# An attention and two-MLP kernel on one core: another mix of tile kinds, other ranks for the planner, and the first shifts all planned

## The chip, the cores and the metric

One NeuronCore of a Trainium2 chip runs the whole kernel. The metric is the device time of one execution in microseconds. Engines: PE (TensorE, products), DVE (VectorE), ACT (ScalarE), POOL (GpSimd) and SP, whose queue issues nearly all DMAs.

## What is computed

Three steps in a row, all in float32: attention with a bucket mask (2 batches, 8 heads, 768 rows, 64 columns a head), a gated MLP with a token shift, and a low-rank token mix followed by a channel MLP.

```python
def _attn_ref(q, k, v, proj):
    ...
    mask = q_bucket[:, :, :, None] == k_bucket[:, :, None, :]
    scores = scale * np.matmul(q, k.transpose(0, 1, 3, 2))
    scores = np.where(mask, scores, -1000000000.0)
    scores = scores - np.max(scores, axis=-1, keepdims=True)
    attn = np.exp(scores)
    attn = attn / (np.sum(attn, axis=-1, keepdims=True) + 1e-09)
    return np.matmul(attn, v).astype(np.float32)

def _moe_ref(x, mu_k, mu_r, w_k, w_v, w_r):
    ...
    xk = mu_k * x + (1.0 - mu_k) * x_prev
    xr = mu_r * x + (1.0 - mu_r) * x_prev
    k = np.maximum(xk @ w_k, 0.0)
    v = k * k @ w_v
    r = 1.0 / (1.0 + np.exp(-(xr @ w_r)))
    return (r * v).astype(np.float32)

def _moe2_ref(x, U, V, w_ch1, w_ch2):
    xt = x.transpose(0, 2, 1)
    h = xt @ U @ V
    u = x + h.transpose(0, 2, 1)
    ch = np.maximum(u @ w_ch1, 0.0) @ w_ch2
    return (u + ch).astype(np.float32)
```

The weights of both MLPs arrive as 64-bit floats and are turned into two float32 parts (high and low) on the chip.

## The kernel before

**Attention.** 16 heads (2 batches of 8) with 6 tiles of 128 rows each, so 96 tiles. For each tile PE makes the scores (`scores`, L514), DVE the row maximum, scale and bias (L524 to L534), ACT the exponentials into a float32 tile `p` (`exps`, L537). Then `p` has to be transposed and multiplied by V. There are two ways:

- The tiles 1 and 4 of each head (`PE_TILES`, L23; 32 in all) are transposed on PE (`flip`, L560), copied out of PSUM in float32 by ACT or DVE (`flip_out`, L568) and multiplied by V in float32 (`weighted`, L573, the product of L581).
- The other 64 are cast to fp16 on POOL or ACT (`part1`, L542), the remainder is subtracted on POOL (`part2`, L546), both parts are transposed by one DMA from SP's queue (`transp`, L554) and multiplied as fp16 (the product of L587, 18 for a tile).

V is scaled by a power of two that is found for a group of `VG` = 4 heads (L470 to L497).

**The order of the attention** comes out of a planner. Every step is an `Op` (L50) with the engines that can do it and a cost on each, the ops it follows, the buffers (`Slot`) it takes and frees, and a rank: its place in the list of tiles plus a number from the table `DUE` (L24). `Plan.order` (L76) plays the ops with these costs; among those that are ready it takes the lowest rank first. The sequence that results is the order in which each engine's instructions are written. Wherever the play leaves PE without work, `idle_products` (L330) adds small products of no use, about 0.85 of the gap's length.

**Handover.** The planned part also holds the conversion of the first `JOBS` = 8 weight tiles, and for batch 0 of the gated MLP the shift `mu * x + (1 - mu) * x_prev` of both halves of r, the products of r, and the shift of the first half of k. A shift is four steps for each of 4 column chunks: `shift_scaled` and `shift_sum` (L705, L720; ACT or DVE, and DVE), `shift_high` (L726, ACT) and `shift_low` (L740, POOL or DVE). The shift of the second half of k is written behind the planned part, between the first unit and the others (L1112, L1113).

**The MLPs.** From there the order is written out by hand. A unit of the gated MLP is `k` (L779, 12 products of 384 columns), `k_act` (L787: relu and square on ACT, a product on POOL), `k_low` (L794, DVE) and, one unit later, `v` (L798, 9 products of 512 columns). With the units run the ticks (L254 to L263): each loads, scales, joins and splits weight tiles, one step of five tiles in a row. The list of tiles is w_r (4), then w_k and w_v in turn (16), U, V in two halves, then the channel MLP's 32. The channel mix (`Channel`, L850) ticks in its first of three groups.

## Time and profile before

| | us |
|---|---|
| median of 3 runs (728.45 to 728.57) | 728.49 |
| the profiled execution | 728.76 |
| its span, first to last instruction | 727.0 |
| PE busy in the span | 707.1 |
| DVE, ACT, POOL busy | 440.6, 385.2, 351.1 |

The span is what the trace covers. Matmul ends are modelled, so a busy PE may still hold small gaps. Times in the rows count from the span's start. In a row of a group "x32 | 47.4, 274" means 32 instructions, 47.4 us during which at least one of them ran, and 274 ns for one from its start to its modelled end.

### The profile page before, as it was taken

The numbers are of one execution on the slowest core, as the hardware profiler recorded it, in microseconds if no ns is written. First come the engines' busy times: TensorE is split into PE (matmuls) and PEld (weight loads), VectorE is DVE, ScalarE is ACT, GpSimd is POOL, SyncE is SP. The second block draws the span as 40 slices with busy tenths as digits, with TensorE's granted clock in tenths as the row PEclk, the third lists the DMA queues.
The fourth block names the chain that finished last, engine by engine and source line by source line (L and its number), as shares of the span: only waits on it lengthen the run. The fifth ranks groups of instructions, "written<-read, shape, count | busy, mean of one in ns | idle before, by whom it ended". The sixth has DMA issues, their size and how long they took to land.

```text
span 727.0 us, 12722 instructions
## 1 busy us (share of the span) xinstructions
PE 707.1 (97%) x4907; PEld 612.1 (84%) x4907; DVE 440.6 (61%) x791; ACT 385.2 (53%) x651; POOL 351.1 (48%) x309
## 2 busy tenths in 40 slices
PE   9899999999999998999999999999999999999997
PEld 8798999999999886889788888778888888888886
DVE  7987888677776656898879978655532111321112
ACT  5887888688878666666478566434421001110100
POOL 5998888787969855566357544613300000000000
PEclk9999999999999999899999999999999999999999
DMA  7899899996987961322013332323201000010001
GB/s 189 194 177 198 190 198 205 167 175 148 174 182 144 208 114 58 116 75 92 2 59 115 116 114 63 125 77 109 65 0 59 1 0 1 1 58 1 0 1 58
DMA packets 140715, 73.23 MB, mean 101 GB/s; under 512 B 116832, under 2 KB 134064, under 8 KB 140656
## 3 DMA queue, kind: packets, MB, share of 16 engines
q1 hardware_dynamic: 140512, 72.24, 43.2%
q8 instruction: 38, 0.62, 0.3%
q10 hardware_dynamic: 144, 0.20, 0.1%
q14 instruction: 21, 0.17, 0.1%
HBM read 37.10 MB, written 3.15 MB: 55 GB/s over the span
## 4 chain that ended last, share of the span: by engine, by line
PE 75%; DVE 8%; POOL 5%; DMA 4%; issue 4%; ACT 3%; SPq 0%; POOLq 0%; ACTq 0%; DVEq 0%
PE ps L807 9%; PE pt L807 9%; PE ps L809 9%; PE pt L809 9%; PE pt L808 9%; PE ps L808 9%; PE pt L581 3%; DMA pT<-p 3%; PE pt L587 3%; PE ps L521 3%; POOL p L180 2%; PE ps L522 2%; PE pt L453 2%; DVE w L180 2%; PE pt L415 1%
## 5 line engine op out<-in xcount | busy, mean ns | idle before, releaser
L882 DVE SCALAR_TENSOR_TENSOR hl<-pt,hl 128x512 fp32r<-128x512 f32 x48 | 33.2, 691 | 170.9 <-ACT hl L881 170.9
L881 ACT ACTIVATE hl<-pt 128x512 fp32r<-128x512 f32 x48 | 28.7, 598 | 185.1 <-PE pt L809 185.1
L809 PE MATMUL ps<-w,hl 128*128 128x512 f32 x288 | 114.3, 397 | 3.3 <-DVE hl L796 3.1
L807 PE MATMUL ps<-w,hl 128*128 128x512 f32 x288 | 115.7, 402 | 0.1
L808 PE MATMUL ps<-w,hl 128*128 128x512 f32 x288 | 113.9, 395 | 0.0
L180 POOL TENSOR_TENSOR cx<-cx,raw 128x512 int32<-128x512 int32 (+2 forms) x55 | 80.4, 1461 | 65.2 <-DVE cx L233 59.2
L180 POOL TENSOR_TENSOR p<-p,p 128x768 f16<-128x768 f32 x64 | 108.0, 1693 | 7.8 <-ACT p L389 5.9
L526 DVE TENSOR_REDUCE nm<-ps 128x1 f32<-128x768 f32 x96 | 90.5, 952 | 17.3 <-PE ps L522 15.9
L540 ACT ACTIVATE p<-ps,nm 128x768 f32<-128x768 f32 x96 | 92.9, 988 | 11.7 <-DVE nm L534 10.3
L807 PE MATMUL pt<-ut,w 128*128 128x512 f32 x192 | 75.6, 394 | 0.0
L809 PE MATMUL pt<-ut,w 128*128 128x512 f32 x192 | 75.0, 391 | 0.0
L808 PE MATMUL pt<-ut,w 128*128 128x512 f32 x192 | 75.0, 391 | 0.0
L521 PE MATMUL ps<-xk,xq 76*128 76x384 f32 x192 | 70.6, 368 | 1.9 <-ACT p L540 1.2
L809 PEld LDWEIGHTS ps<-w,hl 128*128 128x128 f32 x288 | 54.5, 189 | 19.2 <-DVE hl L796 7.1
L807 PEld LDWEIGHTS ps<-w,hl 128*128 128x128 f32 x288 | 54.5, 189 | 14.1 <-issue 1.7
L180 DVE TENSOR_TENSOR w<-cx,w 128x512 fp32r<-128x512 f32 (+2 forms) x52 | 61.2, 1177 | 8.2 <-ACT w L273 7.7
L522 PE MATMUL ps<-yk,yq 128*128 128x384 f32 x192 | 65.1, 339 | 0.0
L808 PEld LDWEIGHTS ps<-w,hl 128*128 128x128 f32 x288 | 54.6, 190 | 10.3
L229 DVE SCALAR_TENSOR_TENSOR raw<-raw 128x512 uint32<-128x512 uint32 (+2 forms) x55 | 54.2, 985 | 0.0
L180 POOL TENSOR_TENSOR sq<-sq 128x384 f32<-128x384 f32 x32 | 32.0, 1000 | 38.2 <-ACT hl L791 37.2
L391 POOL CAST p<-p 128x768 f16<-128x768 f32 x49 | 41.3, 843 | 17.1 <-ACT p L540 15.8
L587 PE MATMUL pt<-v,pT 128*128 128x65 f16 (+1 forms) x1152 | 45.7, 194 | 2.5 <-DMA pT<-p 2.5
(181 smaller groups left out, 1511.5 us busy)
## 6 DMA issues: line engine op xcount, KB each, us to landing
raw<-in_moe_w_ch_dram SPq DMA_DIRECT2D x32, 512.0 KB
raw<-in_moe_w_k_dram SPq DMA_DIRECT2D x8, 512.0 KB
raw<-in_moe_w_v_dram SPq DMA_DIRECT2D x8, 512.0 KB
nk<-in_k_dram SPq DMA_DIRECT2D x16, 192.0 KB
nv<-in_v_dram SPq DMA_DIRECT2D x16, 192.0 KB
nq<-in_q_dram SPq DMA_DIRECT2D x15, 192.0 KB
xk<-yk SPq DMA_DIRECT2D x15, 192.0 KB
xq<-yq SPq DMA_DIRECT2D x15, 192.0 KB
```

Source lines behind the costliest of these rows:

```text
L180: eng.tensor_tensor(out=out, in0=a, in1=b, op=op)
L229: nc.vector.scalar_tensor_tensor(out=raw[:, :, 0], in0=raw[:, :, 1], scalar=0x80000000, in1=raw[:, :, 0], op0=ALU.bitwise_and, op1=ALU.bit ...
L391: (nc.vector if e == "dve" else nc.gpsimd).tensor_copy(dst, src)
L521: nc.tensor.matmul(s_ps[:, j, 0:G], d["xq"][:, qc], d["xk"][:, c], start=True, stop=False)
L522: nc.tensor.matmul(s_ps[:, j, 0:G], d["yq"][:, qc], d["yk"][:, c], start=False, stop=True)
L526: nc.vector.tensor_reduce(out=nm[:, 0:1], in_=tl[n]["s"][:, :, 0:G], axis=AX.XY, op=ALU.max, negate=True)
L540: nc.scalar.activation(p, tl[n].pop("s")[:, :, 0:G], AF.Exp, bias=nm[:, 2:3], scale=nm[:, 1:2])
L587: nc.tensor.matmul(o[:, 0:d], pT[:, part, kt, :], V[:, kt, a, 0:d], start=(kt == 0 and (part, a) == (0, 0)), stop=(kt == NT - 1 and part = ...
L807: nc.tensor.matmul(o, sh, mh, start=first, stop=False)
L808: nc.tensor.matmul(o, sh, ml, start=False, stop=False)
L809: nc.tensor.matmul(o, sl, mh, start=False, stop=last)
L882: nc.vector.scalar_tensor_tensor(out=hl[:, 1], in0=self.o, scalar=0.0, in1=f(hl)[:, 0], op0=ALU.max, op1=ALU.subtract)
```

## The change

The table `MODES` gives each tile of a head a kind, one string for each batch: D goes by DMA as fp16 parts, W is flipped on PE and stays float32, and F is new: flipped on PE, then split out of PSUM into fp16 parts by ACT (high) and DVE (rest) and multiplied as D is. That makes 64 tiles D, 24 W (16 in batch 0, 8 in batch 1) and 8 F (all in batch 1). All ranks of `DUE` are new, and several costs that the planner plays with. Six weight tiles instead of eight are converted in the attention; the ticks take over two tiles earlier in the list, with two more ticks in the channel mix. The V groups are of 2, 2, 4, 4 and 4 heads. The shift of k's second half is planned too; its buffers `xh2` lie where the preparation of the heads had its own, which are given back behind the last scores. The first MLP's units go in the order 0, 1, 2, 3 instead of 0, 2, 1, 3.

```diff
-PE_TILES = (1, 4)
-DUE = {"ld": -28.3, "h": 7, "lo": 111.2, "tr": -11.5, "es": -25.5, "xs": 92.5, "z": -68.8, "bits": 0,
...
+MODES = ("DDWDDW", "DDFDDW")
+DUE = {"ld": -252.8, "h": -1.6, "lo": 280.8, "tr": 133.2, "es": -299.3, "xs": -53.6, "z": -552.9,
...
-JOBS = 8
-VG = 4
+JOBS = 6
+GROUPS = (2, 2, 4, 4, 4)
...
+        scored.append(n)
+        if len(scored) == NH * NT:
+            prep_s.close()
+            late["xh2"] = pool(mix_s, "xh2", bufs=4)
...
+    def mode(n):
+        return MODES[n // (NT * H)][n % NT]
...
+    def flipped(n, part):
+        return tl[n]["pT"][:, part].rearrange("p (j i) c -> p j (i c)", j=NG), tl[n]["f"][:, :, 0:G]
+
+    def flip_part1(n):
+        pT_tile(n)
+        p1, src = flipped(n, 0)
+        nc.scalar.activation(p1, src, AF.Copy)
+
+    def flip_part2(n):
+        p1, src = flipped(n, 0)
+        minus("dve", flipped(n, 1)[0], src, p1)
+        tl[n].pop("f")
...
-        if t in PE_TILES:
+        if mode(n) == "W":
             pT, v = tl[n].pop("pF"), NV[i % len(NV)]
...
+            if kind == "F":
+                p1 = add({"act": 0.83}, lambda e, n=n: flip_part1(n), [fl], n, "f1", [pT_s])
+                got = add({"dve": 0.97}, lambda e, n=n: flip_part2(n), [p1], n, "f2", free=[f_s])
...
-            avs.append(add({"pe": 0.9 if on_pe else 0.62}, lambda e, n=n: weighted(n), [got, v0_of[i] if on_pe else v2], n, "av",
+            avs.append(add({"pe": 1.32 if kind == "W" else 0.56}, lambda e, n=n: weighted(n), [got, v0_of[i] if kind == "W" else v2], n, "av",
...
-    for j, (s, g, c) in enumerate(todo := mx0.todo[0:3 * KD]):
+    for j, (s, g, c) in enumerate(todo := mx0.todo):
         a_s = Slot("sq")
         if c == 0:
-            x_s = [Slot("xh") for _ in range(KD)]
+            far = (s, g) == ("k", 1)
+            x_s = [Slot("xh2" if far else "xh") for _ in range(KD)]
...
-    u1 = [0, 2, 1, 3, *range(4, U1 - 3), U1 - 2, U1 - 3, U1 - 1]
+    u1 = [*range(U1 - 3), U1 - 2, U1 - 3, U1 - 1]
...
-    while mix.todo or mix.begun:
-        shifts(mix, nc.gpsimd if len(mix.todo) % 2 else None)
...
-                if m in (8, 10, 12):
+                if m in (4, 6, 8, 10, 12):
                     tick()
```

How the instructions stand now, at three places. First DVE near the end of the attention, where the last tiles' maxima (`nm<-ps`) are taken. In the rows `pF<-ps` is the float32 copy of a flipped tile, `xs_a` a shift, `y_150` or `y_153` a result of r, `raw` and `cx` a weight tile in conversion, `rl` the row sums. Before:

```order
L526 TENSOR_REDUCE nm<-ps 128x1
L391 COPY pF<-ps 128x768
L530 TENSOR_SCALAR nm<-nm 128x1
L534 TENSOR_SCALAR nm<-nm 128x1
L229 SCALAR_TENSOR_TENSOR raw<-raw 128x512
L233 TENSOR_SCALAR cx<-cx 128x512
L710 MEMSET xs_a 128x1
L391 COPY y_150<-pt 128x512
```

After:

```order
L538 TENSOR_REDUCE nm<-ps 128x1 x2
L738 MEMSET xs_a 128x1
L542 TENSOR_SCALAR nm<-nm 128x1 x2
L546 TENSOR_SCALAR nm<-nm 128x1 x2
L750 SCALAR_TENSOR_TENSOR xs_a<-xT,mu_k,xs_a 128x384 x2
L232 SCALAR_TENSOR_TENSOR raw<-raw 128x512
L236 TENSOR_SCALAR cx<-cx 128x512
L181 TENSOR_TENSOR pT<-ps,pT 128x768
L750 SCALAR_TENSOR_TENSOR xs_a<-xT,mu_k,xs_a 128x384
L622 TENSOR_SCALAR rl<-pt,vsc 128x6
```

`pT<-ps,pT` is the second part of an F tile, which stands here instead of a float32 copy, and k's shifts (`mu_k`) have come in among the last tiles.

Second ACT at the handover. `xT<-pt` is the last copy of the attention's result, `sq<-pt` the relu of a unit of the first MLP, `hl<-sq` its square, `xs_a` and `xh` are shifts, `w`, `cx` and `raw` weights. Before:

```order
L273 ACTIVATE w<-cx 128x512
L790 ACTIVATE sq<-pt 128x384
L791 ACTIVATE hl<-sq 128x384
L224 ACTIVATE cx<-raw 128x512
L225 ACTIVATE raw<-raw 128x512
L716 ACTIVATE xs_a<-xT,omu_k 128x384
L737 ACTIVATE xh<-xs_a 128x384
L716 ACTIVATE xs_a<-xT,omu_k 128x384
L737 ACTIVATE xh<-xs_a 128x384 x3
L273 ACTIVATE w<-cx 128x512
L790 ACTIVATE sq<-pt 128x384
```

After:

```order
L744 ACTIVATE xs_a<-xT,omu_k 128x384
L765 ACTIVATE xh<-xs_a 128x384
L392 ACTIVATE xT<-pt 128x384 x2
L765 ACTIVATE xh<-xs_a 128x384
L276 ACTIVATE w<-cx 128x512
L818 ACTIVATE sq<-pt 128x384
L819 ACTIVATE hl<-sq 128x384
L227 ACTIVATE cx<-raw 128x512
L228 ACTIVATE raw<-raw 128x512
L276 ACTIVATE w<-cx 128x512
L818 ACTIVATE sq<-pt 128x384
```

The shifts that stood between the relu of the first unit and that of the second are now ahead of the first; one high part stands behind the last copy of the attention.

Third DVE in the first MLP, from the eleventh unit's `hl<-sq` on, the low part of a unit's result. `raw` and `cx` are conversions (128x512 a full weight tile, 128x192 the matrix U, 32x384 a half of V), `w<-cx` the split of a tile. Before:

```order
L796 TENSOR_TENSOR hl<-sq,hl 128x384
L180 TENSOR_TENSOR w<-cx,w 128x512
L710 MEMSET xs_a 128x1
L718 TENSOR_SCALAR xs_a<-xT,omu_r 128x127
L718 TENSOR_SCALAR xs_a<-xT,omu_r 128x256
L722 SCALAR_TENSOR_TENSOR xs_a<-xT,mu_r,xs_a 128x384
L229 SCALAR_TENSOR_TENSOR raw<-raw 32x384
L233 TENSOR_SCALAR cx<-cx 32x384
L796 TENSOR_TENSOR hl<-sq,hl 128x384
L180 TENSOR_TENSOR w<-cx,w 128x6x32
L229 SCALAR_TENSOR_TENSOR raw<-raw 32x384
```

After, from the same unit on:

```order
L824 TENSOR_TENSOR hl<-sq,hl 128x384
L181 TENSOR_TENSOR w<-cx,w 128x512
L738 MEMSET xs_a 128x1
L746 TENSOR_SCALAR xs_a<-xT,omu_r 128x127
L746 TENSOR_SCALAR xs_a<-xT,omu_r 128x256
L750 SCALAR_TENSOR_TENSOR xs_a<-xT,mu_r,xs_a 128x384
L232 SCALAR_TENSOR_TENSOR raw<-raw 128x512
L236 TENSOR_SCALAR cx<-cx 128x512
L824 TENSOR_TENSOR hl<-sq,hl 128x384
L181 TENSOR_TENSOR w<-cx,w 128x512
L232 SCALAR_TENSOR_TENSOR raw<-raw 128x192
```

The small matrices come two units later, and full tiles stand in their place.

## Rows read from the trace of the kernel before

**Rows 1.** The page: busy us, share of the span and instructions of each engine.

```profile
PE 707.1 (97%) x4907; PEld 612.1 (84%) x4907; DVE 440.6 (61%) x791; ACT 385.2 (53%) x651; POOL 351.1 (48%) x309
```

**Rows 2.** Windows: PE, PEld, DVE, ACT, POOL busy, clock, DMA share, GB/s.

```profile
0.00:160.00 160.00, 151.69 (x1683) 144.07 (x1684) 129.62 (x292) 124.31 (x195) 133.83 (x134) 1.00 0.93 190
160.00:275.80 115.80, 113.77 (x1234) 104.75 (x1233) 79.67 (x187) 86.98 (x143) 91.64 (x77) 1.00 0.78 156
```

**Rows 3.** The chain of waits, 180 to 262 us: shares by line.

```profile
by line: PE pt L581 16.0%; PE pt L587 13.9%; PE ps L521 12.8%; PE ps L522 11.6%; PE ps L566 8.2%; PE pt L453 7.1%; PE pt L415 5.9%; PE pt L807 5.2%; PE pt L809 4.6%; PE pt L808 4.5%; DVE vpow L489 1.8%; PE pt L332 1.7%; PE pt L616 1.6%; POO
```

**Rows 4.** Groups of instructions, 0 to 282 us: busy us, mean ns, idle before.

```profile
L581 PE MATMUL pt<-nv,pF 128*128 128x65 f32 x384 | 47.4, 274 | 0.0
L587 PE MATMUL pt<-v,pT 128*128 128x65 f16 (+1 forms) x1152 | 45.7, 194 | 2.5 <-DMA pT<-p 2.5
L180 POOL TENSOR_TENSOR xh<-xs_a,xh 128x384 fp32r<-128x384 f32 x12 | 12.4, 1037 | 9.3 <-ACT xh L737 9.3
L391 DVE COPY pF<-ps 128x768 f32<-128x768 f32 x12 | 11.4, 953 | 1.8 <-PE pt L581 0.9 <-PE ps L566 0.7
L737 ACT ACTIVATE xh<-xs_a 128x384 fp32r<-128x384 f32 x13 | 6.7, 519 | 4.0 <-PE pt L809 2.5 <-DVE xs_a L722 1.5
```

**Rows 5.** Timeline of PE, the longest run of filler products: start, length.

```profile
37.10 2.48 PE L332 MATMUL pt<-steady 128*128 128x120 f16 x44
```

**Rows 6.** The scores' second product: durations, first and last start.

```profile
L522 PE MATMUL ps<-yk,yq x192: 332/340/345, 12.1 to 256.9; 128*128 128x384 f32 x192
```

**Rows 7.** Windows behind the first MLP product, columns as in rows 2.

```profile
282.00:287.60 5.60, 3.68 (x14) 2.00 (x12) 4.86 (x7) 3.23 (x8) 3.84 (x3) 1.00 0.00 0
287.60:294.30 6.70, 5.89 (x14) 4.50 (x15) 6.70 (x9) 4.74 (x9) 4.84 (x4) 0.50 0.51 155
...
300.15:340.00 39.85, 39.24 (x195) 34.61 (x195) 36.53 (x53) 28.33 (x54) 26.41 (x22) 1.00 0.28 89
```

**Rows 8.** Timeline of PE, first MLP, first products of runs: start, length.

```profile
275.86 0.42 PE L807 MATMUL pt<-xh,w 128*128 128x384 f32 x1
...
296.01 0.40 PE L807 MATMUL ps<-w,hl 128*128 128x512 f32 x1
...
298.08 0.34 PE L807 MATMUL pt<-xh,w 128*128 128x384 f32 x1
...
300.15 0.39 PE L807 MATMUL ps<-w,hl 128*128 128x512 f32 x1
```

**Rows 9.** Timeline of ACT: relus of the units of the first MLP.

```profile
296.21 0.49 ACT L790 ACTIVATE sq<-pt 128x384 f32<-128x384 f32 x1 [3.74 <-PE pt L809]
...
300.36 0.49 ACT L790 ACTIVATE sq<-pt 128x384 f32<-128x384 f32 x1 [1.48 <-PE pt L809]
...
317.00 0.49 ACT L790 ACTIVATE sq<-pt 128x384 f32<-128x384 f32 x1 [1.47 <-PE pt L809]
...
321.50 0.49 ACT L790 ACTIVATE sq<-pt 128x384 f32<-128x384 f32 x1 [1.40 <-PE pt L809]
...
326.08 0.49 ACT L790 ACTIVATE sq<-pt 128x384 f32<-128x384 f32 x1 [2.22 <-PE pt L809]
...
330.91 0.49 ACT L790 ACTIVATE sq<-pt 128x384 f32<-128x384 f32 x1 [1.97 <-PE pt L809]
```

**Rows 10.** Timeline of DVE and POOL: a weight tile's split, and POOL's addition.

```profile
304.02 0.69 DVE L180 TENSOR_TENSOR w<-cx,w 128x512 fp32r<-128x512 f32 x1
...
317.36 1.80 DVE L180 TENSOR_TENSOR w<-cx,w 128x512 fp32r<-128x512 f32 x1
...
317.06 1.55 POOL L180 TENSOR_TENSOR cx<-cx,raw 128x512 int32<-128x512 int32 x1 [2.02 <-DVE cx L233]
```

**Rows 11.** Waits of PE, 20 to 276 us: us, times, longest.

```profile
PE pt L587 <- DMA pT<-p: 2.5, 4, 1.4
```

**Rows 12.** A window in the channel mix, columns as in rows 2.

```profile
460.00:480.00 20.00, 20.00 (x84) 14.96 (x83) 11.18 (x16) 8.57 (x16) 8.66 (x6) 1.00 0.33 107
```

More of the change, by code (lines that the diff above doesn't have):

```diff
@@ L1021, in lsh_attention_moe_kernel @@
         if j < JOBS + 2:
-            last = add({"dve": 1.75}, lambda e, j=j: conv_bits(j), [last], at, kind)
+            last = add({"dve": 2.2}, lambda e, j=j: conv_bits(j), [last], at, kind)
         if j < JOBS + 1:
@@ L1043, in lsh_attention_moe_kernel @@
         sm = add({"dve": 1.1}, lambda e, p=p: mx0.shift_sum(*p), begun, at, kind)
-        hi = add({"act": 0.53}, lambda e, p=p: hold.append(mx0.shift_high(*p)), [sm, hi and low_of[todo[j - 1]]], at, kind, [x_s[c]])
+        hi = add({"act": 0.53}, lambda e, p=p: hold.append(mx0.shift_high(*p)), [sm, hi and low_of[todo[j - 1]], *(last_s if far else [])],
+                 at, kind, [x_s[c]])
         low_of[p] = add({"pool": 1.05}, lambda e, p=p: mx0.shift_low(*p, hold.pop(), nc.gpsimd), [hi], at, kind, free=[a_s])
```

79 lines of the change are left out of this document (43 added, 36 removed), and 11 rows, old and new, of the table DUE.

## The prediction

> **What bounds the kernel now.** I read the busy shares first, then the windows, the chain of waits, the costliest groups, and last the timeline of the two places the change touches. The product engine PE is busy for 707.1 of 727.0 us [rows 1], so an edit counts where it takes products or holes off PE, and hardly elsewhere. Three stretches matter.
>
> The **attention** runs from 0 to 275.86 us, where the first product of the first MLP starts [rows 2, 8]. Of 275.80 us PE is busy for 151.69 + 113.77 = 265.5 [rows 2], so its holes are 10.3 us. Up to 160 us the engines are all fairly full (PE 151.7, GpSimd 133.8, VectorE 129.6 of 160); from there to 275.8 PE has 113.77 of 115.80 us while VectorE has 79.67, ScalarE 86.98 and GpSimd 91.64 [rows 2]. The chain of waits says the same: from 180 to 262 us the ten lines with the largest shares are all PE's, the float32 weighted sum first with 16.0% [rows 3]. So in the second half products taken away are time taken away.
>
> The **handover** to the MLP is where PE is slowed by something other than its work. From 282.0 to 287.6 us PE is busy for 3.68 of 5.60 us; behind these holes the granted clock stands at 0.50 for 6.7 us, the 1.2 GHz level [rows 7].
>
> The **MLPs and the channel mix** are PE's: one unit of the first MLP has 12 products of 384 columns (298.08 to 300.15, 2.07 us) and 9 of 512 columns (296.01 to 298.08, 2.07 us) [rows 8], 4.14 us together, and ScalarE's relus, one for each unit, come 4.15 us apart [rows 9]. Three of them come 4.50, 4.58 and 4.83 us apart (317.00 to 330.91): there VectorE, which splits the weights, is late.
>
> **Part 1: eight of the 32 flipped tiles are weighted as fp16 parts.** A float32 weighted sum has 12 product rows a tile in the trace, 47.4 us for 32 tiles, 1.48 us each; fp16 parts take 18 short ones, 45.7 us for 64 tiles, 0.71 us each [rows 4]. All eight tiles lie in the second batch, so in the half that PE bounds: 8 x 0.77 = 6.1 us less. The flips stay 32, and the DMA transposes 64. What the eight tiles add is a subtraction on VectorE. A VectorE copy of this size from PSUM takes 0.95 us [rows 4]; I take 1.0 for the subtraction, 8.0 us, and cost it at nothing: VectorE has 36 us free behind 160 us [rows 2]. Without that cover the whole 8.0 us would stand on the path.
>
> **Part 2: order and ranks.** Counted in the order of PE, the filler products up to the end of the attention go from 351 to 335. In the run of 44 one costs 2.48 / 44 = 56 ns [rows 5]; 16 of them are 0.9 us. They move as well: up to the twelfth tile of scores they fall from 230 to 131, behind it they rise from 121 to 204. The smaller first group of V scales lets two fp16 sums and two float32 ones more run before that tile; it costs one more set of small instructions (two tiny products). The planner's real waits are the unknown. The nearest row is the 10.3 us of holes [rows 2]: half of them may go (5.2 us more) or the new order may wait as much longer as parts 1 and 2 save, which makes the attention 0. I keep the 10.3 us, since the stretch that holds most of the work is full already. Attention: -6.1 - 0.9 = **-7.0 us**, from -12.2 to 0.
>
> **Part 3: all first shifts planned.** Before, ScalarE has the four last shifts between the relu of the first unit and that of the second, and VectorE and GpSimd have them likewise; in the new order the relus follow one another with only weight conversions between. From the first product (275.86) to the relu of the fourth unit (296.21) it takes 20.35 us. PE's work up to there is 4 x 2.07 + 2 x 2.07 = 12.4 us, and the relu starts 0.2 us behind the last product (300.15 to 300.36) [rows 8, 9]: 12.6 us. That frees 7.7 us, 3.35 of which is the clock (6.7 us at half rate, [rows 7]). I leave 0.4 us for the first low half of a hidden tile, which the next product waits for in any order: **-7.3 us**. If the holes shrink only so far that the clock stays, it is -3.4; that is the other end. The four shifts aren't free where they go: 4 low parts at 1.04 us and 4 high parts at 0.52 [rows 4], 6.2 us in a row, since the memory they use is free only behind the last scores. Those started at 256.9 [rows 6], 19 us ahead of the MLP, and GpSimd sat idle for 9.3 us ahead of such low parts [rows 4]. That covers them; if it didn't, they would be late by a few us at most and the second unit would wait.
>
> **Part 4: six weight tiles instead of eight in the attention.** The conversions leave engines that don't bound there: nothing gained. But every tick of the first MLP now converts two tiles earlier in the list, so its last ticks hold two full tiles where two small matrices stood. VectorE's units were late by up to 4.83 - 4.15 = 0.68 us [rows 9]; two more such units cost 2 x 0.68 = **+1.3 us**, at least 0. At most all 14 ticks run at the mean of the three late gaps, 4.64: 14 x 0.49 = 6.9 us, of which 1.5 is there already, so +5.4. The two tiles come back as two more ticks in the channel mix, where VectorE has 11.18 us of 20 and PE 20.00 [rows 12]: nothing; uncovered, a tick holds PE up by no more than the 0.68 us above. Two queue entries of SP move with them, behind the transposes; PE waited for those 2.5 us in all [rows 11], so nothing.
>
> **Sum:** 727.0 - 7.0 - 7.3 + 1.3 = 714.0 us of span. The profiled execution took 728.76, 1.76 more than its span, and the median of the runs is 0.27 below it: 714.0 + 1.76 - 0.27 = **715.5 us**.
>
> **The rivals.**
> *The attention isn't shortened.* The holes that PE loses as work are filled by waits for the exponentials, GpSimd or the transposes. For it: up to 160 us GpSimd is at 84% and PE has most of its holes there [rows 2]. Against it: behind 160 us PE is at 98%, and its own work is what goes. Time: 715.5 + 7.0 = 722.5.
> *The handover stays.* The eight low parts at the end of the attention are late, and the holes and the half clock come again. Against it: the 19 us above. Time: 715.5 + 7.3 = 722.8. With the first rival together, 729.8, which is no change.
> *VectorE sets the pace of the whole first MLP.* The same subtraction for a weight took 0.69 us at 304.02 and 1.80 at 317.36, where GpSimd had an addition from 317.06 for 1.55 us [rows 10]. If the two engines meet in every tick, each of the 14 takes 4.64 us: +5.4 instead of +1.3, 719.6. The Trainium skill has a rule for this: SBUF — State Buffer, "SBUF: two separate sides" says that VectorE and GpSimd share a pair of ports as an exclusive lock, and whoever comes second is held for the other's whole instruction. By that rule the row would be 0.69 us and what was left of GpSimd's addition, an estimate of 1.94 by that page; the trace has 1.80 and so agrees in kind. By the rule this rival is the forecast wherever both have such work, and it speaks against converting more in the MLP.
> *Slower than before:* the same lateness, and with it the clock. Holes of 1.9 us within 5.6 us came ahead of the half clock [rows 7]; a stretch of it costs 3.35 us. If PE's holes of 0.49 us a unit bring it back four times, it is 719.6 + 13.4 = 733.0. It decides from the third stretch on (719.6 + 10.05 = 729.7). Against it: the three late units of before, 1.5 us in all, left the clock at 1.00 from 300.15 to 340 us [rows 7].
>
> **How the numbers follow.** Forecast as summed 0.56; attention unshortened 0.18; handover stays 0.07; VectorE paces the MLP 0.08; the two stays together 0.04; slower by the clock 0.07. The low end has the attention at -12.2, the handover at -7.7 and VectorE at 0: 728.5 - 19.9 = 708.6, so 709. The high end takes in the first three rivals (722.5, 722.8, 719.6) and the attention at 0 with some of the VectorE cost: 725. Left out are the last two cases and the tails. A measurement of this kernel tells 0.2%, 1.5 us, from no change: faster 0.56 + 0.18 + 0.07 + 0.08 = 0.89, same 0.04, slower 0.07.
>
> **What would show it.** Part 1: 24 tiles of float32 sums at 1.48 us and 72 of fp16 sums at 0.71. Parts 1 and 2: the first MLP product at 275.9 - 7.0 = 268.9 us. Part 3: no clock of 0.50 behind it, and the fourth relu 13.0 us after that product instead of 20.35. Part 4: relus 4.15 us apart up to the tenth unit, then two or three more gaps of 4.5 to 4.8. I am wrong if the first MLP product comes later than 273 us (then the order's waits grew), if the half clock is still in the handover, or if gaps over 4.5 us begin with the first units.

## The result and the profile after

The changed kernel takes **737.16 us** (median; 733.61 to 738.76) beside 728.71 us of the kernel before on the same chip: a ratio of **1.0103, 95% interval [1.0077, 1.0128]**. The forecast was 715.5 us (709 to 725). It is slower by about 1%, and the prediction was wrong. The profiled execution took 737.47 us with a span of 735.7 us, 8.7 us more than the span before.

The page's busy shares of the kernel after (columns as in [rows 1]) say that PE has as much to do as before, although eight float32 sums have gone:

```profile
PE 707.4 (96%) x4942; PEld 613.5 (83%) x4942; DVE 447.6 (61%) x799; ACT 385.7 (52%) x653; POOL 355.4 (48%) x312
```

Windows of the kernel after (columns as in [rows 2]): the whole attention, one stretch of it, the part of that behind a hole, and the start of the first MLP.

```profile
0.00:288.10 288.10, 269.45 (x2951) 252.57 (x2951) 211.99 (x488) 210.32 (x338) 225.07 (x211) 0.97 0.85 164
...
180.00:200.00 20.00, 17.76 (x158) 17.07 (x157) 10.93 (x23) 12.17 (x19) 14.57 (x14) 0.74 0.80 147
...
186.80:197.60 10.80, 10.73 (x74) 10.73 (x75) 4.29 (x10) 5.70 (x10) 5.84 (x5) 0.54 0.70 137
...
288.10:304.00 15.90, 14.76 (x78) 13.32 (x76) 14.17 (x15) 11.21 (x22) 11.27 (x9) 1.00 0.32 106
```

The first MLP product comes at 288.10 us instead of 275.86 [rows 8]: **+12.2 us where I had -7.0**. PE is busy for 269.45 us of it, so the holes are 18.65 us where they were 10.3 [rows 2], and the granted clock is 0.97 on average where it was 1.00 in both windows [rows 2]: 288.1 x 0.03 = 8.6 us, if all of this time was lost. So -7.0 us of work, +8.4 us of holes and +8.6 us of clock make +10.0 of the 12.2; the other 2.2 us of busy time I can't assign in full. Of the work forecast to go, the filler products did not: the 335 of them are busy for 28.8 us, part of it at half clock, where 351 took 26.7.

PE's costliest groups in this stretch and its longest waits (columns as in [rows 4] and [rows 11]; the groups run to 295 us, the waits to 290), and the fillers' row of the kernel before, 0 to 276 us:

```profile
L615 PE MATMUL pt<-v,pT 128*128 128x65 f16 x1296 | 51.5, 194 | 6.9 <-DMA pT<-p 6.9
L609 PE MATMUL pt<-nv,pF 128*128 128x65 f32 x288 | 37.3, 281 | 0.0
L335 PE MATMUL pt<-steady 128*128 128x120 f16 x335 | 28.8, 241 | 5.5 <-DVE xn L634 2.6 <-DVE nm L542 1.2 <-POOL warm L324 1.0
```

```profile
L332 PE MATMUL pt<-steady 128*128 128x120 f16 x351 | 26.7, 226 | 3.3 <-DVE xn L606 2.0 <-POOL warm L321 1.0 <-DVE rl L594 0.3
```

```profile
PE pt L615 <- DMA pT<-p: 6.9, 5, 2.2
PE pt L335 <- DVE xn L634: 2.6, 2, 2.2
PE ps L529 <- DMA xq<-zt: 2.3, 3, 1.3
```

The waits for the transposes grew from 2.5 us in four [rows 11] to 6.9 us in five. Three waits of the scores for mask copies (`xq<-zt`), which SP issues as well, are new: 2.3 us. One wait for a transpose, in PE's timeline (start, length, and in brackets the idle time ahead), and what SP and GpSimd did meanwhile:

```profile
184.18 0.44 PE L418 MATMUL pt<-ident_r,hl_k 128*128 128x128 f32 x3
186.87 0.72 PE L615 MATMUL pt<-v,pT 128*128 128x65 f16 x18 [2.24 <-DMA pT<-p]
```

```profile
176.21 0.54 SPq L447 DMA_DIRECT2D xk<-yk  x1
176.85 0.54 SPq L447 DMA_DIRECT2D xq<-yq  x1
177.48 1.61 SPq L467 DMA_DIRECT2D xk<-zt  x2
179.14 0.50 SPq L311 DMA_DIRECT2D nk<-in_k_dram  x1
179.69 0.42 SPq L311 DMA_DIRECT2D nq<-in_q_dram  x1
180.16 1.51 SPq L467 DMA_DIRECT2D xq<-zt  x2
181.77 6.58 SPq L567 DMA_TRANSPOSE pT<-p  x3
```

```profile
174.48 1.85 POOL L181 TENSOR_TENSOR p<-p,p 128x768 f16<-128x768 f32 x1
...
181.35 1.64 POOL L181 TENSOR_TENSOR p<-p,p 128x768 f16<-128x768 f32 x1
```

One tile's fp16 parts are finished at 176.33 (174.48 + 1.85), the next tile's at 182.99. SP comes to the first of the two transposes at 181.77, behind eight other issues, and the weighted sum that stands next in PE's order runs at 186.87, 10.5 us behind its parts. Behind this hole of 2.24 us the granted clock is 0.54 for 10.8 us (186.80 to 197.60 above), that is mostly the 1.2 GHz level: up to 5.0 us more (10.8 x 0.46).

At the attention's end, PE and VectorE:

```profile
279.40 1.53 PE L609 MATMUL pt<-nv,pF 128*128 128x65 f32 x12
283.15 3.72 PE L335 MATMUL pt<-steady 128*128 128x120 f16 x37 [2.22 <-DVE xn L634]
286.71 0.50 PE L644 MATMUL pt<-ident,xn 128*128 128x128 f32 x3
```

```profile
280.96 0.23 DVE L622 TENSOR_SCALAR rl<-pt,vsc 128x6 f32<-128x6 f32 x1 [0.98 <-PE pt L609]
281.10 1.30 DVE L750 SCALAR_TENSOR_TENSOR xs_a<-xT,mu_k,xs_a 128x384 f32<-128x384 f32 x1
282.33 0.18 DVE L626 RECIPROCAL rl<-rl 128x6 f32<-128x6 f32 x1
282.54 0.56 DVE L634 TENSOR_TENSOR xn<-pt,rl 128x384 f32<-128x384 f32 x1
```

A shift's sum (L750) stands between the last total and its reciprocal, PE waits 2.22 us, and then 37 filler products, whose bank the normalisation has to read first, run ahead of the last transposes for 3.7 us.

This end weighs as much as the waits for the transposes. The windows from the last product of scores `ps<-xk,xq` to the first MLP product, before and after:

```profile
256.74:275.86 19.12, 17.86 (x216) 15.02 (x216) 9.13 (x24) 11.32 (x21) 10.79 (x9) 1.00 0.47 92
```

```profile
262.33:288.10 25.77, 23.10 (x312) 20.09 (x311) 18.23 (x32) 16.50 (x31) 16.23 (x14) 0.93 0.45 83
```

Of the +12.2 us, 5.6 stand ahead of the last scores and 6.6 behind them, where no sum waits for a transpose. More is left to do there (10 tiles of fp16 sums instead of 6, 2 of float32 instead of 3, 53 fillers instead of 27), PE is idle for 2.7 us instead of 1.3, and the clock is 0.93 instead of 1.00. The sums are only moved there (4 x 0.71 - 1.48 = 1.4 us); the rest is loss.

Behind the attention the change does what was forecast. ScalarE's relus of the units of the first MLP (columns as in [rows 9]):

```profile
302.32 0.49 ACT L818 ACTIVATE sq<-pt 128x384 f32<-128x384 f32 x1 [0.89 <-PE pt L837]
...
323.00 0.49 ACT L818 ACTIVATE sq<-pt 128x384 f32<-128x384 f32 x1 [1.43 <-PE pt L837]
327.64 0.49 ACT L818 ACTIVATE sq<-pt 128x384 f32<-128x384 f32 x1 [1.52 <-PE pt L837]
332.22 0.49 ACT L818 ACTIVATE sq<-pt 128x384 f32<-128x384 f32 x1 [1.89 <-PE pt L837]
337.05 0.49 ACT L818 ACTIVATE sq<-pt 128x384 f32<-128x384 f32 x1 [1.73 <-PE pt L837]
341.62 0.49 ACT L818 ACTIVATE sq<-pt 128x384 f32<-128x384 f32 x1 [2.23 <-PE pt L837]
346.43 0.49 ACT L818 ACTIVATE sq<-pt 128x384 f32<-128x384 f32 x1 [1.95 <-PE pt L837]
```

The fourth relu comes 14.22 us behind the first product (302.32 - 288.10; before 20.35), with a clock of 1.00 there: -6.1 us. (The 1.2 us above the forecast of 13.0 are mostly a wait of PE of 1.14 us, at 294.13, for the first low half of a hidden tile, for which I had left 0.4.) Late units, 4.57 to 4.83 us apart, are five instead of three and exceed 4.15 us by 2.7 us in all instead of 1.5: +1.2. The second MLP is 1.4 us longer; PE waits there once for 1.4 us for a weight that GpSimd splits. 12.2 - 6.1 + 1.2 + 1.4 = 8.7, the difference of the spans.

### The profile page after: what moved, and what is told of

Same layout as the page of the kernel before. It is cut to its first block, busy times and chain, and to the rows that moved or that the text cites. A ratio compares the mean times of both kernels' runs of the same rounds, so it can differ in the third digit from the quotient of the medians.

```text
span 735.7 us, 12806 instructions
## 1 busy us (share of the span) xinstructions
PE 707.4 (96%) x4942; PEld 613.5 (83%) x4942; DVE 447.6 (61%) x799; ACT 385.7 (52%) x653; POOL 355.4 (48%) x312
## 4 chain that ended last, share of the span: by engine, by line
PE 74%; POOL 7%; DVE 7%; DMA 4%; issue 4%; ACT 3%; SPq 0%; POOLq 0%; DVEq 0%; ACTq 0%
PE ps L835 9%; PE ps L837 9%; PE ps L836 8%; PE pt L835 8%; PE pt L837 8%; PE pt L836 8%; PE pt L615 4%; PE ps L529 3%; PE pt L609 3%; PE ps L530 3%; POOL p L181 3%; DMA pT<-p 2%; PE ps L578 2%; PE pt L418 2%; PE pt L335 1%
## 5 line engine op out<-in xcount | busy, mean ns | idle before, releaser
L181 DVE TENSOR_TENSOR w<-cx,w 128x512 fp32r<-128x512 f32 (+2 forms) x52 | 59.3, 1140 | 9.5 <-ACT w L276 9.3
L232 DVE SCALAR_TENSOR_TENSOR raw<-raw 128x512 uint32<-128x512 uint32 (+2 forms) x55 | 59.4, 1080 | 0.0
L615 PE MATMUL pt<-v,pT 128*128 128x65 f16 x1296 | 51.5, 194 | 6.9 <-DMA pT<-p 6.9
L394 POOL CAST p<-p 128x768 f16<-128x768 f32 x50 | 42.9, 866 | 29.6 <-ACT p L552 29.5
L615 PEld LDWEIGHTS <-pT 128*128 128x128 f16 x1296 | 44.7, 98 | 14.5 <-DMA pT<-p 8.2
```

What stands on the lines that cost most here:

```text
L181: eng.tensor_tensor(out=out, in0=a, in1=b, op=op)
L232: nc.vector.scalar_tensor_tensor(out=raw[:, :, 0], in0=raw[:, :, 1], scalar=0x80000000, in1=raw[:, :, 0], op0=ALU.bitwise_and, op1=ALU.bit ...
L394: (nc.vector if e == "dve" else nc.gpsimd).tensor_copy(dst, src)
L615: nc.tensor.matmul(o[:, 0:d], pT[:, part, kt, :], V[:, kt, a, 0:d], start=(kt == 0 and (part, a) == (0, 0)), stop=(kt == NT - 1 and part = ...
```

## The experiments

Every execution lists its span and its mean granted clock. Where the level is half, at most half the time is lost, so span x (1 - clock) is the most that the clock can have cost in it. The table has the median time, its ratio to the kernel before on the same chip with the 95% interval, the mean of that loss over the executions, and the mean of the span without it (6 to 12 executions each; the kernel before: 125). Much of the scatter of one kernel's executions lies in the loss (the changed kernel: 1.5 to 12.5 us); without it the spans of one kernel stand 0.7 to 3.4 us apart (standard deviation), so a mean is good to 1 or 2 us. The true cost is smaller: among the 125 executions of the kernel before the span grows by 0.6 us for each us of this loss (a straight line through them). So the last column takes away too much, and flatters a kernel that loses more: two rows that differ by 5 us of loss may differ by 2 us in this column for that alone. The sum of the last two columns, the mean span, is free of this. Ratios compare on one chip; the last two columns, and medians of different rows, also across chips.

| kernel | median us | ratio to before | lost by clock, at most | span without it |
|---|---|---|---|---|
| before | 728.7 to 732.0 by chip | 1 | 5.4 | 724.1 |
| **changed** | 737.16 | 1.0103 [1.0077, 1.0128] | 7.5 | 727.2 |
| e1: before + fp16 parts | 731.37 | 1.0005 [0.9977, 1.0033] | 5.9 | 724.0 |
| e2: before + handover | 724.62 | 0.9913 [0.9882, 0.9945] | 0.5 | 721.8 |
| e3: before + both | 728.33 | 0.9974 [0.9944, 1.0004] | 4.7 | 722.2 |
| e4: changed, no wait for transposes | 730.01 | 0.9982 [0.9958, 1.0005] | 5.8 | 722.5 |
| e5: before, 8 half sums | 726.52 | 0.9936 [0.9905, 0.9968] | 5.6 | 719.5 |
| e6: changed, later landing in the plan | 750.47 | 1.0275 [1.0243, 1.0307] | 5.4 | 743.6 |
| e7: changed, float32 for fp16 parts | 738.68 | 1.0121 [1.0081, 1.0162] | 5.5 | 732.6 |
| e8: e2, no fillers in the tail | 724.61 | 0.9913 [0.9885, 0.9941] | 2.5 | 720.6 |
| e9: e1, no held fillers | 732.99 | 1.0030 [1.0006, 1.0054] | 8.8 | 722.6 |
| e10: e3, no held fillers | 727.51 | 0.9915 [0.9878, 0.9953] | 3.1 | 720.3 |
| e11: changed, no held fillers | 736.12 | 1.0068 [1.0039, 1.0097] | 13.7 | 720.9 |
| e12: e11, no wait for transposes | 728.00 | 0.9962 [0.9934, 0.9991] | 8.6 | 717.6 |
| e13: before, no wait for transposes | 730.89 | 0.9978 [0.9948, 1.0009] | 6.3 | 723.1 |
| e14: e3, subtraction deferred | 728.62 | 0.9950 [0.9918, 0.9983] | 2.2 | 723.7 |
| e15: changed, transposes in halves | 773.29 | 1.0558 [1.0510, 1.0607] | 30.7 | 740.6 |
| e16: changed, ranks of before | 747.15 | 1.0228 [1.0166, 1.0289] | 6.2 | 740.0 |
| e17: changed, loads from ScalarE | 735.68 | 1.0057 [1.0033, 1.0082] | 11.6 | 722.3 |
| e18: e2, loads from ScalarE | 728.52 | 0.9973 [0.9946, 1.0001] | 5.7 | 721.6 |

Theory 1: the new order places fp16 sums on PE before their transposes have landed; the waits and the half clock behind them are the loss. Theory 2: it is the fillers that stand on the path ("held" in the table are those between a head's last sum and the next head's first, e9 to e12; the tail is what follows the last scores). Against them: the parts themselves don't pay.

### The parts of the change in the old order (e1, e2, e3)

e1 puts one branch ahead of the copy and one in the choice of the weighted sum, and leaves the plan as it is; e2 takes over the plan of all shifts, the two pools and the order of the first MLP; e3 is both.

```diff
     def flip_out(n, e):
+        if as_parts(n):          # n >= NT * H and n % NT == 4
+            nc.scalar.activation(p1, src, AF.Copy)
+            minus("dve", p2, src, p1)
+            return
```

> The kernel before, in its own order, with only the second product tile of each head of batch 1 taken from float32 to two fp16 parts (the rest of the change left out). Theory (part 1 of the change saves TensorE time, the loss lies in the new order): the granted clock of the attention stays near 1 and the time falls by about 6 us, to 722 to 723. Rival (the fp16 parts cost more than they save, because the weighted sum now waits for a cast and a subtraction in a row): 728 or above, with the first MLP product at or behind the 275.9 of before.

> The kernel before, with all sixteen first shifts in the plan (their slots, the pool that opens behind the last scores and the order of the first MLP as in the changed kernel), no fp16 parts and none of the new ranks but the one that the new shifts need. Theory (the handover's gain is real and stands by itself): the fourth relu comes about 14 us behind the first MLP product instead of 20.35, and the time falls by about 6 us, to 722 to 723. Rival (the gain is paid for in the attention, whose VectorE and ScalarE take over the work): first MLP product 4 us or more later than 275.9 and a time of 727 or above.

> The two parts of the runs before together, with the old ranks, the old eight conversion jobs and the old groups of four. Theory (the old order carries both parts, so what made the changed kernel slower is the new order): the two savings add up, 716 to 717. Rival (the two parts hurt each other in the attention, whatever the order): 722 or above.

**e2 came as expected by its ratio**: 0.9913, or 6.4 us (724.62 lies above the 722 to 723 that I named, but on this chip the kernel before takes 730.9). The relu of its fourth unit, the window from its first MLP product, and PE's longest hole in it:

```profile
292.06 0.49 ACT L798 ACTIVATE sq<-pt 128x384 f32<-128x384 f32 x1 [1.48 <-PE pt L817]
```

```profile
276.70:296.00 19.30, 17.12 (x90) 15.63 (x89) 17.41 (x18) 13.14 (x26) 15.08 (x12) 1.00 0.35 110
```

```profile
283.86 0.51 PE L817 MATMUL ps<-w,hl 128*128 128x512 f32 x1 [2.18 <-DVE hl L804]
```

From the first product (276.78) to the fourth relu it takes 15.28 us (I had said about 14), and nothing of the 0.50 of [rows 7] is left, although PE waits for 2.18 us in one piece. Of its gain of 7.2 us in the mean span up to 4.9 us is clock (5.4 to 0.5).

**e1 was a miss**: no gain at all, as its rival said. PE and VectorE of e1 at the place where its attention loses most:

```profile
259.61 0.82 PE L566 MATMUL ps<-ident,p 128*128 128x128 f32 x6
262.78 0.32 PE L332 MATMUL pt<-steady 128*128 128x120 f16 x3 [2.35 <-DVE xn L616]
```

```profile
261.30 0.96 DVE L180 TENSOR_TENSOR pT<-ps,pT 128x768 f16<-128x768 f32 x1 [0.81 <-ACT pT L576]
262.18 0.55 DVE L616 TENSOR_TENSOR xn<-pt,rl 128x384 f32<-128x384 f32 x1
```

The new subtraction (L180) waits for ScalarE's copy at the head of VectorE's queue, the normalisation (L616) stands behind it, and three fillers, whose bank it reads, hold PE for 2.35 us. In the 3.3 us behind it the granted clock is 0.55. e3 shows the same hole of 2.35 us; it went as its rival said (728.33, forecast 716 to 717), and is slower with the parts than with the handover alone, by the clock: 4.7 us lost instead of 0.5, with the same span without it. And yet e3 is well below the changed kernel, which has the same two parts: what else the change brings (order, ranks, places of the tiles, conversions) costs some 9 us.

### No wait for the transposes (e4, e12, e13)

```diff
-    o[:, 0:d], pT[:, part, kt, :], V[:, kt, a, 0:d],
+    o[:, 0:d], pT[:, part, kt, :] if own else steady, V[:, kt, a, 0:d],   # own: not a transposed tile
```

> The changed kernel, order unchanged, but the weighted sums of the 64 transposed tiles take the constant ones tile as their weights instead of the tile that the transposing DMA wrote (the transposes still run, nobody waits for them; the output is not the reference's). Theory 1 (TensorE's order places these sums before their transposes have landed; the wait and the half clock behind it are the main loss): no wait for the transposes is left, the granted clock of 180 to 200 us goes from 0.74 to near 1, the first MLP product comes at 273 to 280 instead of 288.1, and the time falls by 8 to 15 us, to 722 to 729. Theory 2 (the loss is at the end of the attention: fillers that stand behind the last heads' normalisation): nothing changes ahead of the tail, 734 to 737. Rival 3 (the clock falls whatever the waits are): the waits vanish, but 180 to 200 us keeps a granted clock under 0.85, and 729 to 733. Rival 4 (other waits of the new order, for scores' inputs and for the casts, take up what is set free): under 3 us gained, 734 or above.

> The changed kernel without these fillers and with the transposed tiles' sums taking constant weights, so that nobody waits for a transpose (the output is not the reference's, as in the run without these waits, which came to 730.0). Theory (the two losses are apart and add up): 725 to 727, and with that within 2 us of 725, where the kernel before stands with the handover alone. Rival (they are one and the same loss, since each starts the other by the half clock): 729 or above.

> The kernel before, order unchanged, with the transposed tiles' sums taking constant weights (as was done to the changed kernel, which became 7 us faster by it). Theory (the waits for the transposes are a fault of the new order and cost the old one little): at most 3 us less than the kernel before. Rival (they cost the old order as much, so they don't explain the difference between the two): 5 us or more less.

**Theory 1 holds for the waits, not for the whole loss.** The changed kernel becomes 7 us faster by the medians and 9 by the ratios (6.4 us in the mean span, up to 1.7 of it clock), and without the held fillers 8 us (e12: 728.0, between the two ranges I had named). The kernel before gains 1.6 us by its ratio, with an interval that takes in no change, as expected. So these waits are the new order's. But e4's 730.0 lies above the 722 to 729 of Theory 1, and its first MLP product comes at 283.4 instead of 273 to 280: its last scores come at 257.8 (before 256.7), and the 25.6 us behind them are nearly the 25.8 of the changed kernel. The stretch from 180 to 200 us, now in e4:

```profile
180.00:200.00 20.00, 20.00 (x261) 18.74 (x259) 16.27 (x41) 15.67 (x25) 19.76 (x17) 1.00 0.94 168
```

PE is busy for 20.00 instead of 17.76 us, at 1.00 instead of 0.74. Without its waits the new order stands about where the old one with the same parts stands: 722.5 (e4) and 722.2 (e3) without the clock, 728.3 and 726.9 in the mean span. The rival that the clock falls whatever the waits are isn't dead: in e4 another hole, 1.97 us of scores that wait for ScalarE at 108.8, is followed by half clock (0.74 over 100 to 120 us). So the clock can fall behind any hole, but doesn't behind each: e2's of 2.18 us, above, has none behind it. In the kept profiles 26 of 31 holes of 1.9 us or more have half clock begin in them or within 2.1 us behind them.

### Where PE paces (e5), and the parts undone in the new order (e7)

e5 takes three of the six key tiles in the eight sums; e7 does the eight tiles in float32 again, in the changed kernel's own order.

```diff
-            for kt in range(NT):
+            some = NT // 2 if n >= NT * H and t == 4 else NT
+            for kt in range(some):
```

```diff
     def flip_part1(n):
+        return flip_out(n, "act")
     def flip_part2(n):
+        return
-        if mode(n) == "W":
+        if mode(n) in "FW":
```

> The kernel before, order unchanged, but the float32 weighted sums of the second product tile of each head of batch 1 take three of their six key tiles (six matmuls of twelve, 8 x about 0.69 us = 5.5 us of TensorE work taken away and nothing put in its place on any engine; half of these sums is left out of the result). Theory (in batch 1 TensorE is not what paces the attention; work taken from it comes back as waits, and this is why the fp16 parts alone gained nothing): scores 48 to 96 come at most 2 us earlier than before, time 726 to 731 beside 728 to 731 of the kernel before. Rival (TensorE paces, and the fp16 parts gained nothing because the added subtraction on VectorE and the longer chain from the flip to the sum hold the score banks): about 5 us faster.

> The changed kernel in its own order, with the eight tiles of fp16 parts done as float32 tiles again (one copy by ScalarE, no subtraction on VectorE, the weighted sum in float32). Theory (the fp16 parts bring nothing in this order, since what they take from TensorE comes back as waits): within 3 us of the changed kernel, 734 to 740. Rival (they do save their 6 us here): 741 to 744. Second rival (they cost, by holding a score bank through copy and subtraction): 733 or below.

My theory fell in e5: work taken from PE is time, 4.7 us of the 5.5 by the ratio (0.9936), and in the profiles the last scores come 4 us earlier. (726.5 is in the theory's range only because the kernel before takes 731.3 on this chip.) So PE does pace the second half, as the prediction had it, and in the old order something that the parts add eats their gain. In the new order they seem to save: without the clock's loss the span with float32 is 5.4 us longer (732.6 and 727.2), in the mean span 3.4, in the medians 1.5. These are six executions each, on two chips, and the intervals of the ratios meet (1.0121 and 1.0103), so this isn't shown. For e7 the time was in the first theory's range; whether for its reason is open.

### Fillers (e8, e9, e10, e11)

e8 leaves them out behind the last scores, the others (the edit below) between a head's total and the next head's first weighted sum.

```diff
     def idle_products(n):
-        for _ in range(n):
+        for _ in range(0 if held else n):      # total: held.append(i); weighted: held.clear()
```

> The kernel before with the handover alone (the run that came to 724.6), without any fillers behind the last scores. Theory 2 (fillers behind the last scores stand on the path: two groups of 17 to 19 between the last normalisation and the last transposes, about 2.1 us, and a filler's wait of 0.6 us for a normalisation): 2 to 3 us less, 721.5 to 722.5, with the first MLP product about 2.5 us earlier. Rival (they keep the clock up): the clock falls to half behind 270 us, and the time is the same or more.

> The kernel before with the fp16 parts alone (the run that came to 731.4, no gain), and no filler products between a head's total and the next head's first weighted sum (there the fillers' bank waits for the normalisation to be read). Theory (the parts' 6 us are given back at 262.8, where three fillers wait 2.35 us for a normalisation that stands in VectorE's queue behind the new subtraction, and in the half clock behind that wait): the wait is gone, the granted clock of 260 to 280 us goes from 0.91 to 1.0, and the time falls by 4 to 6 us, to 725 to 727. Rival (the parts' chain holds the score banks all through batch 1): the same time, 730 or above. Rival 2 (without these fillers the idle gaps are longer and the clock falls elsewhere): the same or more, with a clock under 0.95 in another stretch ahead of 276.

> The handover and the fp16 parts with the old ranks (the run that came to 728.3), without the same fillers. Theory: both savings are kept, 718 to 721, faster than the run of the handover alone (724.6). Rival: 725 or above.

> The changed kernel, its order unchanged, without the same fillers (about 140 fewer). Theory (of the 12 us lost in the attention the end's 2.2 us wait, its 3.7 us of fillers behind the last normalisation and part of the half clock are theirs, the waits for the transposes are not): 3 to 5 us less, 732 to 734, first MLP product at 283 to 285, and the waits for the transposes (6.9 us) still there. Rival (they are gap filling only): 736 or above.

**Theory 2 is a miss for the time, and the table shows why.** In e11 some 143 fillers go (143 x 56 ns = 8.0 us); the span without the clock's loss falls by 6.3 us, and the loss rises by 6.2: the mean span stays (734.6 and 734.7), and the first MLP product is earlier (283.6), as expected. e8: -1.2 and +2.0. e9: the hole at 262.8 is gone, -1.4 and +2.9. So leaving the fillers out on the path gains nothing, and more half clock comes without them; how much of the one pays for the other isn't told apart, since the loss is an upper bound. e8, e9 and e11 went as their rivals for the time said. Only e10 has a lower ratio than its partner (0.9915 beside 0.9974, with intervals that meet); its median of 727.51 beside 730.18 is 0.9963 and lies in the rival's range. It is no lower than the handover alone.

### The planner's numbers (e6, e16)

```diff
-                got = add({"sp": 2.2}, ..., n, "T", [pT_s], [c_s], issue=1.7)
+                got = add({"sp": 2.2}, ..., n, "T", [pT_s], [c_s], lag=1.6, issue=1.7)
```

e16 puts the old `DUE`, and the `GROUPS = (4, 4, 4, 4)` that belongs to it, into the changed kernel.

> The changed kernel with one number of its planner altered: a transposing DMA counts as landed 1.6 us later (about 5.6 us from issue to landing, as the traces show, instead of about 4). The order is planned anew. Theory 1 (the order counts the transposes as landed too early): the waits for the transposes fall from 6.9 us to under 2.5 us, no half clock in the attention behind such a wait, and the time comes to what the run without these waits gave, 727 to 732. Rival (the sums, moved later, hold up something else: the p slots, the last sums of a head, the spare bank): 735 or above, with the waits elsewhere.

> The changed kernel with the ranks of the kernel before (and its four groups of four value heads, which these ranks need), all else as changed: tile kinds and places, six conversion jobs, the planner's new durations, the handover. Theory A (the new ranks are what costs): 726 to 731. Theory B (ranks fit only the durations for which they were chosen, as the run with the longer transposes said; the old ones in the new planner give an order with longer holes): 745 or above, with more filler products than the 345 of the changed kernel. Between, 732 to 740: the ranks make no difference and the new tile places or durations do.

Both were far slower: e6 missed the time of Theory 1 and went as its rival, e16 went as its Theory B (some 185 filler products more). In e6 the waits for the transposes do fall to 0.6 us, but the order has a stretch in which every engine but PE is nearly empty, and PE runs many of the order's 285 additional fillers (335 in the changed kernel):

```profile
240.00:260.00 20.00, 19.02 (x214) 16.16 (x213) 5.79 (x11) 9.74 (x21) 6.86 (x7) 1.00 0.11 24
```

Ranks belong to the durations for which they were chosen. The old ranks in the new planner lose as the new ones do with one duration corrected, so neither run says what the right ranks would give.

### Where the transposes are late (e15, e17, e18) and the subtraction's place (e14)

e15 issues each transpose as two, one for each part; e17 and e18 issue the loads of k, q and v from ScalarE's queue; e14 puts the subtraction of e3 into VectorE's queue only ahead of the next score bank or of its own sum.

```diff
-        nc.sync.dma_start_transpose(out=pT..., in_=p12...)
+        for a in (0, 1):
+            nc.sync.dma_start_transpose(out=pT[:, a], in_=p12[:, a].rearrange("p g c -> p (g c)"))
```

```diff
-        (eng or nc.sync).dma_start(out=t, in_=src[b, h]...)
+        (eng or nc.scalar).dma_start(out=t, in_=src[b, h]...)
```

```diff
-            minus("dve", p2, src, p1)
+            late_sub.append(lambda: minus("dve", p2, src, p1))   # run ahead of psum_s() and of its own sum
```

> The changed kernel in its own order, with every transposing DMA issued as two, one for each fp16 part. Theory (TensorE waits because a transpose lands 4.4 to 6.7 us behind its issue, at DMA queues that are 80 to 100 per cent busy, so how it is cut changes little): waits for the transposes within 3 us of the 6.9 before, 734 to 740. Rival (a shorter transfer lands sooner): waits under 3 us, 732 or below. Second rival (SP's queue, with two issues for one, becomes late): 745 or above.

> The changed kernel, TensorE's order unchanged, with the 47 loads of k, q and v heads issued from ScalarE's queue instead of SP's (SP spends about 256 of 288 us of the attention on issuing, 30 of them on these loads). Theory (a transpose is late because it stands in SP's queue behind loads and copies, as at 176.2 to 181.7 us, where eight other issues stand ahead of one whose data are ready since 176.3): waits for the transposes under 5 us instead of 6.9, 731 to 735. Rival (it is late for GpSimd's subtraction or for the busy DMA engines, so SP's queue doesn't matter): waits unchanged, 736 or above. Second rival (ScalarE, which now stands still until a load's buffer is free, delays the exponentials): 740 or above, with TensorE waiting for ScalarE.

> The kernel before with the handover alone (724.6), with the same loads issued from ScalarE's queue. Theory (the old order waits little for its transposes, so it gains little): 723 to 726. Rival (ScalarE is held up by the loads' waits): 728 or above.

> Handover and fp16 parts with the old ranks (the run of 728.3), with the new subtraction put into VectorE's queue only ahead of the next score bank that is taken or of its own weighted sum, so that a normalisation no longer stands behind it. Theory (in the old order the parts lose their gain because the subtraction waits for ScalarE's copy at the head of VectorE's queue, with the normalisation and the row maxima behind it): span without the clock's loss 718 to 720 instead of 722.2, time 722 to 725. Rival (the longer chain holds the score banks wherever the subtraction stands): 727 or above.

**e15** went as the second rival: 5.6% slower. PE's waits for transposes in e15, and SP's time for one transpose (ns: least, median, most) in the changed kernel and for one half in e15:

```profile
PE pt L615 <- DMA pT<-p: 14.4, 14, 3.6
```

```profile
L567 SPq DMA_TRANSPOSE pT<-p x64: 1310/1738/3607, 20.6 to 274.0; - x64
```

```profile
L570 SPq DMA_TRANSPOSE pT<-p x116: 1209/1238/2753, 18.9 to 286.6; - x116
```

A half costs SP 1.24 us where a whole costs 1.74 (medians). Added up over its timeline, SP issues for 242 of 288 us in the changed kernel (my expectation's 256 counted some twice) and for 264 of 290 in e15. It was as full before, 232 of 276 us. Nor is the average transpose later or tighter in the new order: from the finished parts to SP's issue it takes 3.0 us in the mean in both kernels, and to the sum 11.1 us before and 11.4 after. So the waits are those of five single tiles, by what stands ahead of what there. **e17** emptied the queue by 47 loads. The hole at 184.5 to 186.9 is gone, but the sum of the waits stays at 6.6 us, nearly all in one, at another place; PE, SP and GpSimd of e17:

```profile
198.48 1.16 PE L615 MATMUL pt<-v,pT 128*128 128x65 f16 x18 [6.34 <-DMA pT<-p]
```

```profile
189.50 1.74 SPq L467 DMA_DIRECT2D xk<-zt  x2
191.28 2.05 SPq L467 DMA_DIRECT2D xq<-zt  x2
193.51 6.43 SPq L567 DMA_TRANSPOSE pT<-p  x2
```

```profile
190.07 3.27 POOL L181 TENSOR_TENSOR p<-p,p 128x768 f16<-128x768 f32 x2
```

PE is at this sum from 192 us. GpSimd has its first part by 191.7, SP issues at 193.51 behind four mask copies, and it lands 5 us later. So even without SP's queue the sum would have waited: GpSimd, SP and the landing each have a share. e17's waits went as the first rival said, its time lies between the theory and that rival. It is 3 us faster than the changed kernel by the ratios, whose intervals meet, and 1.5 us by the medians; in the mean span 0.8 (4.9 us without the clock's loss, of which the clock takes up to 4.1 back). In the traces SP's queue is a part of the cause; in the time it isn't shown. The Trainium skill (DMA: Bandwidth & Descriptors, "Issuing engines are not separate DMA queues") says that DMAs started on several engines run on the same DMA engines, so that only the time to start them is saved; the waits' sum of 6.6 us beside 6.9 fits that but doesn't test it, as GpSimd was late too. e18 lost 4 us to e2, as its rival said; its profile has one wait of 3.6 us for VectorE's row maxima, at 31 us, whose cause isn't followed here. e14 changed nothing that can be told (0.9950 beside 0.9974), as its rival said, though the hole of 2.35 us is gone.

## Why the prediction was wrong

**Part 1's price was right, its worth was not.** The 24 float32 tiles left take 37.3 us, 1.55 each with the half clock in it, the 72 fp16 sums 51.5 us, 0.715 each, as forecast (1.48 and 0.71). The eight subtractions cost 7.6 us of VectorE. That PE paces the second half is shown by e5. But "I cost it at nothing" fell: e1 has PE's saving and no gain, and its trace has the subtraction in front of a normalisation for which PE waits. 36 us of free time on VectorE didn't keep the operation off PE's path there, since it stands in a queue. That this hole eats the gain isn't shown: e9 and e14 take it away and get no faster that can be told. In Part 2 the 0.9 us of fillers didn't come either (26.7 to 28.8 us).

**"I keep the 10.3 us" is the step that failed.** I reasoned that a stretch full of work has no room for more holes. An order fixed beforehand makes its own holes wherever a result comes later than the planner counted: 18.65 us, and the end behind the last scores became 6.6 us longer. I had named the waits for the transposes (2.5 us [rows 11]) and bounded them by what the parts save, so that the attention could not become longer than before; nothing in the rows gave that bound. e4 and e13 show them: 7 us by the medians in the new order, and 1.6 in the old, not told from none. At 176 to 182 us the changed kernel's SP queue has copies ahead of a ready transpose, which I priced for Part 4's two queue entries only.

**The clock was a rival in the wrong place.** I allowed half clock in the MLP's late units, at 0.07. It came in the attention: up to 8.6 us there by the window's 0.97, as much as the holes grew (8.4). My own row gave the price (3.35 us for a stretch [rows 7]); I didn't ask what a longer wait in the attention would bring with it.

**Part 3 was right**: the fourth relu 14.22 us behind the first product (forecast 13.0; the first low half took 1.14 us instead of 0.4), no half clock behind it; -6.1 us, and e2 has it alone at 0.9913. The four last shifts came ahead of the MLP, but a shift's sum for k stands ahead of the normalisation for which PE waits 2.22 us. (The "other end" of this part, -3.4, should be -7.3 + 3.35 = -3.95; nothing rests on it.)

**Part 4 was right**: +1.2 us for two more late units (forecast +1.3), gaps of 4.57 to 4.83 us. The rival by which VectorE is held in every tick isn't what happened; the relus are 4.13 to 4.14 us apart from the fourth (302.32) up to 323.00. The tiles moved to the channel mix, costed at nothing, show in one wait of 1.4 us.

In the sum: -7.0, -7.3, +1.3 and 0 were forecast, and +12.2, -6.1, +1.2 and +1.4 measured. What is shown: the waits for the transposes are the new order's and worth about 7 us with their clock, which is as much as the kernel is slower than before; the handover is worth 6; leaving out the fillers gains nothing. What stays open: the longer end of the attention (without the held fillers it is 21.7 us instead of 25.8 in e11's profile, with no gain in the time); what ranks chosen with the real delays would give; and where the parts' gain goes in the old order. e12, without these waits and the held fillers, is still 12.5 us above the forecast, up to 8.6 of it clock. The fastest kernel with the whole result is the kernel before with the handover alone (e2, e8).

## What to carry to other kernels

Where a planner or a table sets the order of an in-order engine, price the change of order by the results that come latest: take the time from finished input to first use in the trace (here GpSimd's subtraction, SP's queue and 5 us of landing) and look what stands in the queue ahead of each. Before an added operation is costed at nothing for an engine's free time, look what stands behind it in the queue (e1: a normalisation, and 2.35 us of TensorE); here that hole alone didn't explain the loss. And price a hole in TensorE's work with the half clock that may follow it: of the handover's 6.1 us up to 3.35 were clock [rows 7].

## What the hardware showed that I had not expected

- Holes of 2.24 us (changed kernel, 184.6 to 186.9) and 2.35 us (e1, 260.4 to 262.8) were followed by a granted clock of 0.54 over 10.8 us and 0.55 over 3.3 us. But one of 2.18 us (e2, 281.7 to 283.9) was not: the clock is 1.00 from 276.7 to 296. Behind the hole of 2.22 us ahead of the MLP, 37 fillers took 3.72 us, 101 ns each, where 44 took 56 ns each before [rows 5].
- Executions of one kernel differ in how much half clock they have: the loss, span x (1 - clock), was 1.5 to 12.5 us in the changed kernel, and 0 to 1.4 in e2. The span itself grew by only 0.6 us for each us of it (125 executions of the kernel before).
- A transposing DMA of 128 x 1536 fp16 holds SP's queue for 1.74 us (median) and one of half its size for 1.24, so the same data in halves takes 2.5 us of the queue: 64 x 0.74 = 47 us more.
